# A three-stage transformer kernel on one core: second layer by block products, with its final sums folded into the last evictions, x differences kept in DRAM, w2's sums issued one per step, and weight conversion in order of use

## The chip, the cores and the metric

The kernel runs on one core of a Trainium2 chip. The metric is the device time of one execution in microseconds (us). Engines are named as in the profile: PE is TensorE (PEld its weight loads), DVE is VectorE, ACT is ScalarE, POOL is GpSimd, SP is SyncE, which here only issues DMAs; SPq is SP's queue of DMA issues.

## The reference, cut to what matters

Three parts follow each other; each one's output is the next one's input x.

```python
# 1 attention with random features, q k v of (4, 8, 576, 64)
x = num / den                                   # -> (2304, 512)
# 2 eight experts, dense, weighted by a balanced P (8 Sinkhorn turns on exp(x @ w_gate))
for e in range(8):
    h = np.maximum(x @ w1[e], 0.0)              # (2304, 512) @ (512, 1024)
    ye = h @ w2[e]                              # (2304, 1024) @ (1024, 512)
    out += P[:, e:e+1] * ye
# 3 one layer pair, weights given as float64
h = x @ w_in                                    # (2304, 512) @ (512, 2048)
out = (h - np.tanh(h)) @ w_out                  # (2304, 2048) @ (2048, 512)
```

## The kernel before

Every float32 operand is split into a high and a low part (`split`: ACT casts the high part, DVE or POOL subtracts it to get the low part), and a product is three matmuls of 128 rows by 384 or 512 columns. PE's program runs through the stages (0, 0), (0, 1), (0, 2) of part 2 and (1, 0), (1, 1), (1, 2) of part 3, each over 768 tokens. Stage (0, 0) loads w1 and w2, forms their sums and splits, and stores them in DRAM (`st1`, `st2`); later stages load them back.

**Stages (0, 1) and (0, 2)** take 32 steps Q each ("quads", numbered g = 0 to 63 over both). A quad multiplies 256 columns of one expert's w1 with x by seven block products (`product`, L1116: six matmuls each) and, between them, does the second layer of the quad before (`group`, L1281), also by seven block products: 42 matmuls on either side, 84 in a quad. `quad7` (L1186) calls `between(k)` after product k. That runs `slot(7 * g + k)`, in which the preloads of the next slot, the matmuls of this one, their evictions and the pieces `post(k)` are issued in this order; then it calls `tick` twice, which moves the background work on by a step: `weights` (loads, sums and splits of weights), `xops` (the next stage's x) and `convert`.

Each of the seven running sums `seven` (`xacc`) has two halves d. A group of matmuls adds to one half in one of two ways. With `act`, ACT preloads the half into a PSUM bank one slot ahead (L1286, named Y), the matmuls add to it, and ACT copies it back (L1304). Without, the matmuls start from zero (named X) and DVE adds the bank to the half (L1308). PSUM has four banks for groups (`lbank`) here. After the last quad of a stage `join` (L1316) adds the seven sums to the four blocks of the stage's output with DVE and POOL (L1321) and SP writes them to DRAM (`put`, L1325).

The second layer's left operand h is made on DVE (`gated`), cast by ACT (L1203) and its low part subtracted by POOL (L1206). In stage (0, 1) the first 32 quads also need fresh splits of w2's sums: `sums_of` (L208) issues four POOL operations in a row (L213 to L216).

**x** of the next stage is prepared by `xops` (L334): four blocks are loaded, differences formed by DVE (L361) and seven units split into a ring of eight tiles, most of them by DVE (L91), while the last quad of the stage frees them. At the end of stage (0, 0), `x2` (L1471) turns the output round in eight pieces: PE transposes, ACT copies to a tile of the ring `xo` (three buffers, also used by `keep`), and ACT issues the DMA.

**Conversion** of the float64 weights of part 3 (`convert`, L1058) takes jobs of 128 by 256 elements, the whole of w_in first, then w_out: a load by SP, six DVE operations, one of ACT and one of POOL, and a store. It runs in stage (0, 0), halts, and goes on in stage (0, 2). `fetch` (L189) loads converted weights only once all jobs are done (L192).

Of the kernel before, what the change touches and what calls it, by code (L numbers as in the profile page):

```python
# [20 lines left out]
def performer_moe_kernel(ctx, tc, q, k, v, omega, wg, w1, w2, win64, wout64, out):  # L21
# [6 lines left out]
    P = 128  # L28
# [38 lines left out]
    pd = dp.tile([NTT * E, P], F32, name="pd")  # L67

# [12 lines left out]


# [72 lines left out]
    def second_units(R):  # L155
# [6 lines left out]
        return units[:4] + [(0, R)] + units[4:] + [(6, R)] if r == NQ - 1 else units  # L162

    def weights():
# [3 lines left out]
        for Q in range(NQ):  # L168
            e, q = divmod(Q, NQE)
            jobs.append(("q", Q, lambda e=e, q=q: load_quad(e, q)))  # L170
            for f in (2 * q, 2 * q + 1):
                jobs.append(("s", 2 * Q + f % 2, lambda e=e, f=f: load_slab(w2[e][f * P : (f + 1) * P, :])))
        for g in range(NG + 1):
            jobs.append(("c", g, None))
        for s in range(NSB):
            for g in range(NGM):
                for f in range(g * GF, (g + 1) * GF, 2):
                    jobs.append(("i", 0, lambda f=f: load_win(f)))
                for f in range(g * GF, (g + 1) * GF):
                    jobs.append(("s", -1, lambda f=f: load_slab(wout32[f * P : (f + 1) * P, :])))  # L180
        ahead = []

        n_last = 3 * NGM * GF // 2 * NSB
# [5 lines left out]
        def fetch():  # L189
            while jobs and len(ahead) < 5:  # L190
                k = jobs[0][0]
                if len(jobs) <= n_last and not converted:  # L192
# [8 lines left out]
                k, a, f = jobs.pop(0)  # L201
# [6 lines left out]
        def sums_of(raws):  # L208
# [4 lines left out]
            G.tensor_tensor(s1, a21, a22, ALU.add)  # L213
            G.tensor_tensor(s2, s1, a11, ALU.subtract)
            G.tensor_tensor(s4, a12, s2, ALU.subtract)
            G.tensor_tensor(s3, a11, a21, ALU.subtract)  # L216
            return {1: s2, 2: s3, 3: s1, 5: s4}

        while ahead or jobs:
# [25 lines left out]
            elif k == "c":  # L245
                fresh = 0 < a <= NQ
                if a == 1:
                    send(9)
                    raws = slabs(0)
                    for _ in range(4):  # L250
                        yield 1
                    src = sums_of(raws)
                    yield None
                if fresh:
                    if a < NQ:
                        raws = slabs(a)
                    for _ in range(3):
                        yield 1
# [4 lines left out]
                for i in range(max(7, len(units))):  # L263
# [18 lines left out]
                    if fresh and (g < 0 or g == R and o in (1, 2, 3, 5)):  # L282
                        split(u, src[o], nc.vector if o == 2 else G)
                        store(st2[R][:, o], u)
# [5 lines left out]
                if fresh:  # L290
                    if a < NQ:
                        src = sums_of(raws)
# [36 lines left out]
    w2p, converted = [], []  # L329
# [4 lines left out]
    def xops():  # L334
        nx = 0
        order = []
        for k, (kind, s) in enumerate(stages):
# [18 lines left out]
            if kind == 0:  # L356
# [9 lines left out]
                subs = [do((0, 0), (0, 1), (0, 0)), do("t2", (1, 1), (0, 0)), do((0, 1), (1, 1), (0, 1))]  # L366
                last = [do("t2", (1, 0), "t2")]
                tiles = [(0, 0), "t2", (0, 1), (0, 0), (1, 0), (1, 1), "t2"]
                if opening:
                    load(0, 0)  # L370
                    load(1, 0)
                    yield None
                    plan = [0, 4, "rest", *subs[:2], 1, 3, subs[2], 2, 5, *last, 6]
# [18 lines left out]
                else:  # L392
                    for i, j in ((0, 0), (0, 1), (1, 1), (1, 0)):
                        load(i, j)
                    for _ in range(3):
                        yield None
                    seq = [(m, {0: subs, 1: last}.get(m)) for m in range(7)]
            else:
# [4 lines left out]
                seq = [(m, None) for m in range(4)]  # L403
            for m, then in seq:
                while not (len(order) < NX or order[len(order) - NX] in spentx):
                    yield 1
                unit(nx + m, b[tiles[m]], G if kind and m % 2 or not kind and m == 4 else V)
                yield None
                for f in then or ():
                    f()  # L410
                    yield None
            nx += len(seq)

    xdone = set()
# [6 lines left out]
    with ExitStack() as actx, tc.manual_schedule():  # L421
# [364 lines left out]
        for i in range(NUN):  # L786
            for r, items in enumerate(PLAN):
# [19 lines left out]
                if (i == 2 or i > 4) and r == SPL:  # L807
                    next(wprep, None)
# [900 lines left out]
```

## Time and profile before

| | us |
|---|---|
| median of 3 runs | 2172.45 (2170.06 to 2173.23) |
| profiled execution | 2173.33, of which the trace's span is 2171.5 |
| PE busy in the span | 2050.5 (94%) |
| PEld busy | 1908.8 (88%) |
| DVE busy | 1633.4 (75%) |
| POOL busy | 1498.8 (69%) |
| ACT busy | 1273.0 (59%) |

The stages follow each other in time: attention to about 190 us, stage (0, 0) to about 690, stage (0, 1) to about 1240, stage (0, 2) to about 1730, part 3 to the end. A busy share is a mean over all of them.

### The profile page before, as it was taken

The page shows a single profiled execution, that of the slowest core. Times are in us where ns is not written, and L with a number is a line of the kernel's source. Part 1 is how long each engine was busy: PE and PEld are TensorE (multiplying, and loading weights), DVE is VectorE, ACT ScalarE, POOL GpSimd, SP SyncE. Part 2 cuts the span into 40 slices and gives each one's busy share as a digit, 9 for nine tenths or more (in the row PEclk, how much of TensorE's full clock was granted, in tenths as well). Part 3 has the DMA queues.
Part 4 walks back from the last instruction along what each step waited for, and adds up shares of the span by engine and source line. Part 5 has one row for each costly group of instructions (what it writes and reads, how often), then busy time and mean ns, then how long its engine had stood idle before and what let it go on. Part 6 is the DMA issues. An engine that isn't in the chain of part 4 may idle for free.

```text
span 2171.5 us, 37317 instructions
## 1 busy us (share of the span) xinstructions
PE 2050.5 (94%) x11408; PEld 1908.8 (88%) x11408; DVE 1633.4 (75%) x3190; ACT 1273.0 (59%) x3110; POOL 1498.8 (69%) x1868
## 2 busy tenths in 40 slices
PE   9998999999999899999999869999999869999999
PEld 7776988899998799898998869899999869989998
DVE  8884868989876465666566657676777679999997
ACT  7883333344442355555555526666666668888885
POOL 7875877787873577777777657567676787666552
PEclk9999999999999899999999979999999989999999
DMA  6538778788865588787887578878888613222310
GB/s 171 132 101 291 270 258 288 256 285 278 281 244 192 181 289 284 254 295 264 259 296 263 197 239 277 308 265 285 304 290 301 238 70 106 80 96 78 106 41 34
DMA packets 343671, 475.03 MB, mean 219 GB/s; under 512 B 71200, under 2 KB 165040, under 8 KB 343472
## 3 DMA queue, kind: packets, MB, share of 16 engines
q1 hardware_dynamic: 337872, 466.04, 64.0%
q10 hardware_dynamic: 5600, 6.61, 0.9%
q8 instruction: 91, 1.49, 0.3%
q14 instruction: 108, 0.88, 0.1%
HBM read 332.48 MB, written 140.06 MB: 218 GB/s over the span
## 4 chain that ended last, share of the span: by engine, by line
PE 67%; DVE 9%; POOL 8%; DMA 8%; issue 4%; ACT 3%; SPq 1%; POOLq 0%; ACTq 0%; DVEq 0%
PE l L1429 18%; PE Y L1294 12%; PE b L1122 11%; PE e L1122 8%; PE a L1122 7%; PE p L1390 7%; PE X L1294 5%; DMA u<-st 2%; DMA st<-y 2%; POOL tmp L529 1%; POOL h L1206 1%; POOL eq L689 1%; DMA xd<-xo 1%; DVE seven L1308 1%; DVE t L1410 1%
## 5 line engine op out<-in xcount | busy, mean ns | idle before, releaser
L1429 PE MATMUL l<-v,h 128*128 128x512 f32 x2016 | 482.2, 392 | 2.0 <-ACT h L1133 0.8
L1429 PEld LDWEIGHTS l<-v,h 128*128 128x128 f32 x2016 | 376.4, 188 | 78.3 <-ACT h L1133 1.6
L1294 PE MATMUL Y<-h,y 128*128 128x384 f32 x1812 | 391.4, 344 | 47.8 <-POOL h L1206 32.2
L1294 PEld LDWEIGHTS Y<-h,y 128*128 128x128 f32 x1812 | 328.3, 194 | 58.4 <-POOL h L1206 39.0
L1122 PE MATMUL b<-x,u 128*128 128x384 f32 x1728 | 353.9, 340 | 17.1 <-DVE t L1216 16.3
L1304 ACT COPY seven<-Y 128x384 f32<-128x384 f32 x364 | 175.2, 481 | 311.0 <-PE Y L1294 309.5
L1206 POOL TENSOR_TENSOR h<-t,h 128x384 fp32r<-128x384 f32 x224 | 230.7, 1030 | 150.0 <-ACT h L1203 117.3
L1122 PEld LDWEIGHTS b<-x,u 128*128 128x128 f32 x1728 | 311.0, 191 | 22.9 <-DVE t L1216 16.6
L1206 POOL TENSOR_TENSOR h<-h,h 128x384 fp32r<-128x384 f32 x192 | 204.4, 1068 | 103.7 <-ACT h L1203 76.0
L1122 PE MATMUL a<-x,u 128*128 128x384 f32 x1152 | 234.6, 338 | 6.1 <-DVE h L1136 4.3
L1122 PE MATMUL e<-x,u 128*128 128x384 f32 x1152 | 238.3, 342 | 1.9 <-DVE t L1249 1.9
L1390 PE MATMUL p<-x,u 128*128 128x384 f32 x1152 | 212.6, 339 | 14.9 <-DVE seven L1308 8.9
L1390 PEld LDWEIGHTS p<-x,u 128*128 128x128 f32 x1152 | 205.0, 190 | 19.5 <-DVE seven L1308 9.2
L1122 PEld LDWEIGHTS a<-x,u 128*128 128x128 f32 x1152 | 205.0, 190 | 7.7 <-DVE h L1136 4.6
L1122 PEld LDWEIGHTS e<-x,u 128*128 128x128 f32 x1152 | 208.5, 193 | 2.4 <-DVE t L1249 2.4
L1294 PE MATMUL X<-h,y 128*128 128x384 f32 x876 | 191.1, 340 | 8.8 <-ACT h L1203 5.1
L91 POOL TENSOR_TENSOR v<-rs,v 128x256 fp32r<-128x256 f32 x176 | 143.9, 845 | 63.5 <-ACT v L88 53.5
L1418 POOL TENSOR_TENSOR h<-t,h 128x384 fp32r<-128x384 f32 x94 | 98.5, 1047 | 117.5 <-ACT h L1417 114.3
L1286 ACT COPY Y<-seven 128x384 f32<-128x384 f32 x364 | 176.3, 488 | 0.3
L1294 PEld LDWEIGHTS X<-h,y 128*128 128x128 f32 x876 | 157.1, 191 | 12.9 <-ACT h L1203 5.4
L1308 DVE TENSOR_TENSOR seven<-X,seven 128x384 f32<-128x384 f32 x256 | 135.7, 548 | 36.8 <-PE X L1294 36.7
L1203 ACT CAST h<-t 128x384 fp32r<-128x384 f32 x224 | 115.4, 515 | 62.8 <-POOL t L1259 30.0
(243 smaller groups left out, 3857.9 us busy)
## 6 DMA issues: line engine op xcount, KB each, us to landing
u<-st SPq DMA_DIRECT2D x448, 256.0 KB, 5.1
y<-st SPq DMA_DIRECT2D x336, 256.0 KB, 4.9
st<-u SPq DMA_DIRECT2D x224, 256.0 KB, 3.7
rs<-in_moe_w_dram SPq DMA_DIRECT2D x128, 256.0 KB, 4.3
st<-y SPq DMA_DIRECT2D x128, 256.0 KB, 5.6
st<-v SPq DMA_DIRECT2D x96, 256.0 KB, 5.0
rq<-in_moe_w_dram SPq DMA_DIRECT2D x32, 512.0 KB, 4.6
rqi<-win SPq DMA_DIRECT2D x24, 512.0 KB, 4.3
```

Source lines behind the costliest of these rows:

```text
L91: eng.tensor_tensor(dst[:, 1, i : i + w], src[:, i : i + w], dst[:, 0, i : i + w].bitcast(F32), ALU.subtract)
L529: nc.gpsimd.tensor_tensor(tmp[:, c], t[:, c], t[:, c], ALU.mult)
L1122: nc.tensor.matmul(ps[:, :TB], u[:, wi, c], x[:, xi, c], start=(start and m == 0), stop=(stop and m == 5), skip_group_check=True,)
L1203: nc.scalar.copy(H[k][:, 0], src)
L1206: eng.tensor_tensor(H[k][:, 1], src, H[k][:, 0].bitcast(F32), ALU.subtract)
L1286: nc.scalar.copy(cell[0], xacc[i][:, d])
L1294: nc.tensor.matmul(ps, uw[i, g][0][:, wi, d * P : (d + 1) * P], Hs[g][i][:, hi], start=(n == 0 and not cell), stop=(n == 3 * len(gs) - 1), ...
L1304: nc.scalar.copy(xacc[i][:, d], ps)
L1308: nc.vector.tensor_tensor(xacc[i][:, d], ps, xacc[i][:, d], ALU.add)
L1390: nc.tensor.matmul(ps, u1[f + i][:, wi, c], ux[state["x0"] + 2 * t + i][:, xi, c], start=(m == 0), stop=(m == 11))
L1418: nc.gpsimd.tensor_tensor(lo, s, hi.bitcast(F32), ALU.subtract)
L1429: nc.tensor.matmul(ps, hh[f][0][:, hi, t : t + P], u2[n + f][:, wi], start=(f == 0 and i == 0), stop=(f == len(hh) - 1 and i == 2),)
```

## The change

- **Second layer.** In `second_layer`, groups of half 0 and all first groups now go through ACT (`act` true): 194 groups that were X become Y, and rows of ACT go from 3137 to 3517, of DVE from 3192 to 3014. The last quad's groups get a list `outs`: their evictions are DVE additions of the PSUM bank and another running sum, so `join` only writes to DRAM. The 16 additions over 768 columns in the two joins (4 on DVE, 12 on POOL) go, and 40 over 384 columns on DVE come. The order of groups in the last quad changes.
- **Splits of h.** `hsplit(5)` and `hsplit(0)` are issued one product earlier.
- **w2's sums.** `sums_of` returns its four POOL operations, which are issued one per step. The low part of a split (`lower`) is issued one step after its cast.
- **x.** The four differences of stages (0, 1) and (0, 2) are formed early, stored in DRAM (`dd`), and the seven units are loaded one by one into the ring of five tiles; units 1, 3 and 5 are split by POOL. For each of these stages SP issues four more stores and seven more loads of 384 KB. `x2` uses this ring of five in place of `xo`.
- **Conversion.** Jobs come in the order in which part 3 uses them, and `fetch` waits only for the jobs that a load needs. In stage (0, 2) sixteen steps pass between the first load and its first use, and the pace is 26 steps in 32 ticks in place of 22.
- Two small matmuls of the gate use another ring of PSUM banks; attention sends stores at some of its steps.

```diff
-        if act and not first:
+        if (act or outs) and not first:
             at(t)[0].append(pre)
...
             def evict():
-                if act:
+                if outs:
+                    for x, y in outs:
+                        nc.vector.tensor_tensor(xacc[x][:, d], ps, xacc[y][:, d], ALU.add)
+                elif act:
                     nc.scalar.copy(xacc[i][:, d], ps)
...
-        def one(k, i):
+        def one(k, i, outs=()):
             first = r == 0
-            group(t + k, i, [R], 1, i in upper, first, False)
-            group(t + k, i, [R], 0, False, first, True)
+            group(t + k, i, [R], 1, first or i in upper, first, False, outs)
+            group(t + k, i, [R], 0, True, first, True, outs)
...
+        if r == NQ - 1:
+            one(1, 0)
+            two(2, 3, 5, [(5, 0)])
+            two(3, 6, 4, [(4, 0)])
+            one(4, 3, [(3, 0), (5, 5)])
+            one(5, 2, [(2, 0), (3, 3)])
+            one(7, 1, [(5, 5), (3, 3), (2, 2)])
+            one(8, 6, [(6, 2)])
+            join(s, t)
+            return
...
-        at(t + 4)[2].append(add(5, 3, G))
-        at(t + 5)[2].append(add(3, 2, G))
-        at(t + 6)[2].extend((add(4, 0, G), put(4, 0, 0)))
-        at(t + 7)[2].extend(
-            (add(1, 0, V), add(5, 1, V), put(5, 0, 1), add(3, 1, G), put(3, 1, 1), add(2, 1, G))
-        )
-        at(t + 8)[2].extend((add(6, 2, G), put(6, 1, 0), lambda: xdone.add((1, s))))
+        at(t + 6)[2].append(put(4, 0, 0))
+        at(t + 7)[2].extend((put(5, 0, 1), put(3, 1, 1)))
+        at(t + 8)[2].extend((put(6, 1, 0), lambda: xdone.add((1, s))))
...
         between(4)
+        hsplit(5, h22)
         product(b, 5, False, True, last)
...
         between(5)
-        hsplit(5, h22)
+        hsplit(0, h11)
         product(e, 6, False, True, last)
...
+                if a < NQ:
+                    src, todo = sums_of(raws)
+                    for f in todo:
+                        f()
                         yield None
...
+                for i, (dst, x, y) in enumerate(parts):
+                    minus(dst, x, y)
+                    yield None
+                    nc.sync.dma_start(dd[s - 1][i], b[dst])
...
+                    unit(nx + m, b[m], G if m % 2 else V)
+                    yield None
+                    if 0 < m < 3:
+                        fill(m + 4)
...
-                if len(jobs) <= n_last and not converted:
+                if jobs[0][3] > converted[0]:
                     break
...
         nx = ld()
-        yield
+        for _ in range(16 if fine else 1):
+            yield
...
-        x = xtp.tile([P, TB], F32, tag="xo", name="xo2", bufs=3)
+        while xbusy:
+            next(xprep)
+        x = xtp.tile([P, 2, TB], F32, tag="x", name="xo2")[:, 0]
```

**Place 1: POOL in quad 18 of stage (0, 1).** Rows h_18_5 and h_18_0 are low parts of h (the second number is its block), rows y are low parts of fresh w2 units, rows s are w2's sums. Before:

```order
L1206 TENSOR_TENSOR h_18_5_12923<-h_18_12867,h_18_5_12923 128x384
L91 TENSOR_TENSOR y_12941<-s,y_12941 128x256
L213 TENSOR_TENSOR s<-rs 128x256
L214 TENSOR_TENSOR s<-s,rs 128x256
L215 TENSOR_TENSOR s<-rs,s 128x256
L216 TENSOR_TENSOR s<-rs 128x256
L1206 TENSOR_TENSOR h_18_0_12949<-h_18_12887,h_18_0_12949 128x384
L1206 TENSOR_TENSOR h_18_3_13005<-t_18_12979,h_18_3_13005 128x384
```

and of the change:

```order
L1253 TENSOR_TENSOR h_18_5_12996<-h_18_12955,h_18_5_12996 128x384
L1253 TENSOR_TENSOR h_18_0_13017<-h_18_12978,h_18_0_13017 128x384
L241 TENSOR_TENSOR y_12913<-s,y_12913 128x256
L241 TENSOR_TENSOR y_13037<-s,y_13037 128x256
L238 TENSOR_TENSOR s<-rs 128x256
L238 TENSOR_TENSOR s<-s,rs 128x256
L238 TENSOR_TENSOR s<-rs,s 128x256
L1253 TENSOR_TENSOR h_18_3_13093<-t_18_13069,h_18_3_13093 128x384
```

The block h_18_0 has moved ahead of the sums; three sums and two low parts of y now stand ahead of h_18_3.

**Place 2: DVE at the start of stage (0, 2).** The names b, e, a with 32 to 34 are that quad's first-layer banks, t and h its temporaries, cw are the conversion's. Before, the conversion's first operation stands in the second quad of the stage:

```order
L1321 TENSOR_TENSOR seven_9437<-seven_9437,seven_9436 128x768
L1321 TENSOR_TENSOR seven_9441<-seven_9441,seven_9437 128x768
L1248 TENSOR_TENSOR t_32_15779<-b_32_15544,h_32_15660 128x384
L1249 TENSOR_TENSOR t_32_15780<-h_32_15630,b_32_15544 128x384
L1078 TENSOR_SCALAR cw_False<-r_36_15784 128x256
L1216 TENSOR_TENSOR t_7_33_15754<-b_33_15751,t_7_33_15753 128x384
```

and of the change, a quad later:

```order
L1263 TENSOR_TENSOR t_7_34_16089<-b_34_16086,t_7_34_16088 128x384
L1268 TENSOR_TENSOR t_7_34_16090<-b_34_16086,t_7_34_16088 128x384
L1269 TENSOR_TENSOR t_7_34_16090<-e_34_16087,t_7_34_16090 128x384
L1246 SCALAR_TENSOR_TENSOR h_34_16154<-t_7_34_16090,pb_0_15051 128x384
L1126 TENSOR_SCALAR cw_False<-r_36_15933 128x256
L1129 TENSOR_SCALAR cw_False<-cw_False 128x256
L1246 SCALAR_TENSOR_TENSOR h_34_16185<-a_34_16085,pb_0_15051 128x384
```

The first cw row, which waits for the load r, has moved from ahead of t_7_33 to behind three rows of quad 34.

**Place 3: ACT in the last quad of stage (0, 2).** Y and seven are the preloads and evictions named above (block, then half), h are casts. Before:

```order
L1286 COPY Y_2_1_21769<-seven_9438 128x384
L1304 COPY seven_9439<-Y_3_1_21738 128x384
L1203 CAST h_62_1_21780<-h_62_21574 128x384
L1286 COPY Y_1_1_21794<-seven_9437 128x384
L1304 COPY seven_9438<-Y_2_1_21769 128x384
L1203 CAST h_62_6_21805<-t_62_21783 128x384
```

and of the change:

```order
L1333 COPY Y_2_1_22011<-seven_9464 128x384
L1333 COPY Y_2_0_22013<-seven_9464 128x384
L1354 COPY seven_9465<-Y_3_1_21979 128x384
L1354 COPY seven_9465<-Y_3_0_21981 128x384
L1250 CAST h_62_1_22023<-h_62_21822 128x384
L1333 COPY Y_1_1_22036<-seven_9463 128x384
L1333 COPY Y_1_0_22038<-seven_9463 128x384
L1354 COPY seven_9464<-Y_2_1_22011 128x384
L1354 COPY seven_9464<-Y_2_0_22013 128x384
L1250 CAST h_62_6_22048<-t_62_22026 128x384
```

A slot with two groups now has two preloads and two evictions ahead of its cast, where it had one of each.

## Rows read from the trace of the kernel before

**Rows 1.** Chain of waits, PE: line, releaser: us in total, times, longest.

```profile
PE Y L1294 <- POOL h L1206: 32.2, 15, 3.4
PE b L1122 <- DVE t L1216: 16.3, 1, 16.3
PE Y L1294 <- ACT Y L1286: 14.9, 7, 5.0
PE p L1390 <- DVE seven L1308: 8.9, 1, 8.9
```

**Rows 2.** Windows: us, busy us (instructions) PE, PEld, DVE, ACT, POOL, PEclk, DMA, GB/s.

```profile
690.00:740.00 50.00, 42.12 (x212) 38.42 (x211) 23.67 (x45) 14.46 (x33) 18.20 (x21) 0.88 0.56 175
740.00:1205.00 465.00, 435.05 (x2397) 426.77 (x2396) 291.07 (x547) 255.67 (x626) 345.49 (x396) 0.97 0.82 274
1205.00:1280.00 75.00, 50.63 (x239) 48.36 (x238) 42.46 (x68) 25.40 (x56) 45.70 (x39) 0.77 0.60 203
1280.00:1450.00 170.00, 164.91 (x934) 163.81 (x933) 124.43 (x238) 106.73 (x252) 113.10 (x114) 0.98 0.80 274
1450.00:1700.00 250.00, 249.86 (x1441) 249.34 (x1440) 187.51 (x371) 166.99 (x399) 173.27 (x175) 1.00 0.84 296
1700.00:1785.00 85.00, 61.75 (x316) 58.50 (x315) 58.23 (x83) 53.53 (x127) 66.06 (x62) 0.90 0.38 129
```

**Rows 3.** Waits of PE from 740 to 1205 us.

```profile
PE Y L1294 <- POOL h L1206: 28.7, 14, 2.7
PE X L1294 <- DVE seven L1308: 0.4, 2, 0.2
```

**Rows 4.** Timeline of POOL: start, us, engine, line, operation [idle before, releaser].

```profile
879.64 0.74 POOL L213 TENSOR_TENSOR s<-rs 128x256 f32<-128x256 f32 x1
...
882.64 1.71 POOL L1206 TENSOR_TENSOR h<-h,h 128x384 fp32r<-128x384 f32 x1
```

**Rows 5.** Timeline of PE at the same place.

```profile
884.41 0.62 PE L1294 MATMUL Y<-h,y 128*128 128x384 f32 x2 [2.72 <-POOL h L1206]
...
885.92 2.12 PE L1294 MATMUL Y<-h,y 128*128 128x384 f32 x6
...
890.60 1.20 PE L1122 MATMUL a<-x,u 128*128 128x384 f32 x6
```

**Rows 6.** Timeline of ACT at the change to stage (0, 1).

```profile
707.77 0.48 ACT L1478 COPY xo<-x 128x384 f32<-128x384 f32 x1 [3.13 <-DMA xd<-xo]
...
717.87 0.48 ACT L1478 COPY xo<-x 128x384 f32<-128x384 f32 x1 [1.55 <-DMA xd<-xo]
```

**Rows 7.** Timeline of PE there.

```profile
716.00 0.69 PE L1294 MATMUL X<-h,y 128*128 128x384 f32 x1 [5.05 <-ACT h L1203]
...
720.93 2.29 PE L1122 MATMUL e<-x,u 128*128 128x384 f32 x6 [1.89 <-DVE t L1249]
```

**Rows 8.** Timeline of DVE at the change to stage (0, 2).

```profile
1267.94 0.29 DVE L1078 TENSOR_SCALAR cw_False<-r 128x256 f32<-128x256 f32 x1 [15.98 <-DMA r<-in_moe_w_in_dram]
```

**Rows 9.** Waits of SP's queue from 1200 to 1310 us.

```profile
SPq L1325 <- POOL seven L1321: 22.5, 2, 11.4
```

**Rows 10.** Timeline of PE at the change to part 3.

```profile
1734.90 4.58 PE L1390 MATMUL p<-x,u 128*128 128x384 f32 x12 [5.86 <-ACT u L88]
```

**Rows 11.** Timeline of DVE there.

```profile
1750.76 0.55 DVE L1410 SCALAR_TENSOR_TENSOR s<-t,s 128x384 f32<-128x384 f32 x1
...
1759.27 2.18 DVE L1410 SCALAR_TENSOR_TENSOR t<-t,t 128x384 f32<-128x384 f32 x1
...
1765.06 4.46 DVE L1321 TENSOR_TENSOR seven<-seven,seven 128x768 f32<-128x768 f32 x2
```

**Rows 12.** Groups of ACT and DVE, 1450 to 1700 us: busy us, mean ns, idle before.

```profile
L1286 ACT COPY Y<-seven 128x384 f32<-128x384 f32 x119 | 57.9, 487 | 0.0
L1304 ACT COPY seven<-Y 128x384 f32<-128x384 f32 x120 | 57.7, 481 | 65.8 <-PE Y L1294 65.8
...
L1308 DVE TENSOR_TENSOR seven<-X,seven 128x384 f32<-128x384 f32 x53 | 29.1, 549 | 8.5 <-PE X L1294 8.4
```

More of the change, by code (lines that the diff above doesn't have):

```diff
@@ L248, in weights @@
                     send(9)
[L249 to L253, printed above, removed]
+                if a < NQ:
+                    raws = slabs(a)
                 if fresh:
[L255 to L258, printed above, removed]
+                    yield 1
+                    yield 1
+                late = []
                 R = a - 1
@@ L282, in weights @@
                     if fresh and (g < 0 or g == R and o in (1, 2, 3, 5)):
-                        split(u, src[o], nc.vector if o == 2 else G)
-                        store(st2[R][:, o], u)
+                        nc.scalar.copy(u[:, 0], src[o])
+                        if late:
+                            late.pop()()
+                        late.append(lambda o=o, u=u: lower(R, o, u, src[o]))
                         yield None
@@ L327, in weights @@
             fetch()
-    w2p, converted = [], []
+    w2p = []
     ux = {}
@@ L372, in xops @@
                     yield None
+                    subs = [do((0, 0), (0, 1), (0, 0)), do("t2", (1, 1), (0, 0)), do((0, 1), (1, 1), (0, 1))]
+                    last = [do("t2", (1, 0), "t2")]
+                    tiles = [(0, 0), "t2", (0, 1), (0, 0), (1, 0), (1, 1), "t2"]
                     plan = [0, 4, "rest", *subs[:2], 1, 3, subs[2], 2, 5, *last, 6]
@@ L391, in xops, with fill @@
                     continue
[L392 to L397, printed above, removed]
+                for i, j in ((0, 0), (0, 1), (1, 1), (1, 0)):
+                    load(i, j)
+                for _ in range(3):
+                    yield None
+                parts = (
+                    ("t2", (0, 1), (0, 0)), ((0, 1), (1, 1), (0, 1)), ((1, 1), (1, 1), "t2"), ((1, 0), (1, 0), (1, 1))
+                )
+                for i, (dst, x, y) in enumerate(parts):
+                    minus(dst, x, y)
+                    yield None
+                    nc.sync.dma_start(dd[s - 1][i], b[dst])
+                yield None
+                yield None
+                side = lambda i, j: src[:, i, :, t0 + j * TB : t0 + (j + 1) * TB]
+                from_ = [side(0, 0), dd[s - 1][2], dd[s - 1][1], dd[s - 1][0], side(1, 0), side(1, 1), dd[s - 1][3]]
+                def fill(m):
+                    b[m] = xtp.tile([P, 2, TB], F32, tag="x", name=f"xm{m}")
+                    nc.sync.dma_start(b[m], from_[m])
+                xbusy.append(True)
+                for m in range(5):
+                    fill(m)
+                    yield None
+                for m in range(7):
+                    while not (len(order) < NX or order[len(order) - NX] in spentx):
+                        yield 1
+                    unit(nx + m, b[m], G if m % 2 else V)
+                    yield None
+                    if 0 < m < 3:
+                        fill(m + 4)
+                    yield None
+                xbusy.clear()
+                nx += 7
+                continue
             else:
@@ L402, in xops @@
                 tiles = [(0, 0), (1, 0), (0, 1), (1, 1)]
-                seq = [(m, None) for m in range(4)]
-            for m, then in seq:
+            for m in range(4):
                 while not (len(order) < NX or order[len(order) - NX] in spentx):
                     yield 1
-                unit(nx + m, b[tiles[m]], G if kind and m % 2 or not kind and m == 4 else V)
+                unit(nx + m, b[tiles[m]], G if m % 2 else V)
                 yield None
[L409 to L412, printed above, removed]
+            nx += 4
+    xbusy = []
     xdone = set()
@@ L1279, in slot, with group @@
         plan.pop(t)
-    def group(t, i, gs, d, act, first, last):
+    def group(t, i, gs, d, act, first, last, outs=()):
         cell = []
@@ L1367, in second_layer @@
             one(6, 6)
-        elif r == NQ - 1:
-            one(3, 0)
-            one(8, 6)
-            join(s, t)
     pbs = []
```

83 lines of the change are left out of this document (46 added, 37 removed).

## The prediction

> **What bounds the kernel now.** I read the waits of PE first. PE is busy for most of the span, so what can be won is its idle time and the time in which it ran slowly. Four lines lead [rows 1]: groups of the second layer wait 32.2 us in 15 places for POOL's low parts, one product waits 16.3 us for DVE, groups wait 14.9 us for ACT's preloads, and the first products of part 3 wait 8.9 us for DVE's last evictions.
>
> Then the windows, to see where these lie [rows 2]. From 1450 to 1700 us, inside stage (0, 2), PE is busy 249.86 of 250 us and 1441 matmuls are recorded: 0.1735 us each. That is what PE does when nothing is late, and 84 of them make a quad of 14.6 us. From 740 to 1205, inside stage (0, 1), 2397 matmuls of the same kind take 465 us, 0.1940 each: 2397 x 0.0205 = 49 us are lost. The changes of stage lose more per us: 239 matmuls in 1205 to 1280 are worth 41.5 of 75 us (33 lost), and PE idles 7.9 us in 690 to 740 and 23.3 us in 1700 to 1785. The part from 1280 to 1450 loses 8.
>
> A stall costs more than itself. After the 2.72 us wait at 884.41 a group's six matmuls take 2.12 us, where 1.20 is usual [rows 5], and the granted clock of that stretch's window is 0.97, at the change to stage (0, 2) 0.77 [rows 2]: PE works at the lower of its two levels for some us after each. In 740 to 1205 the waits sum to 29.1 us [rows 3], so of the 49 some 20 are the clock's.
>
> **w2's sums and the earlier splits of h (term D).** Ahead of the stall at 884.41 POOL works through the four sums, from 879.64 on, and starts the late h only at 882.64 [rows 4]; PE's group starts when that h is done [rows 5]. This repeats in every second quad, 14 times in the window [rows 3]: the block of h that two quads share (h_0) stands behind the sums. The order shows it moved ahead of them, and cast a product earlier. The sums are now ahead of h_3, whose consumer comes some slots later: two low parts and three sums at 0.74 us [rows 4] are 3.7 us, nearly two slots of 2.08 us (14.6 / 7), and each h takes POOL about 1 us more. I see room, but little: POOL is busy 345.5 of the 465 us, so over 28.5 quads 12.1 us each, 83% of 14.6. Bounds: 49 us if the stage runs as (0, 2) does, 10 us if h_3 and its followers are late instead. I take 39, four fifths, nearer to the upper end because the moved row is the one that PE waited for.
>
> **DMA.** A faster stage must move its bytes faster. 465 us at 274 GB/s are 127.4 MB [rows 2]; the stage's eleven new x transfers of 384 KB add 4.3 MB. In 426 us that is 309 GB/s; the highest mean that a full-speed window shows is 296. If 296 were the ceiling, the window could not be shorter than 131.7 MB / 0.296 = 445 us, and D would be 20. The Trainium skill, "DMA: Bandwidth & Descriptors", section "Where 436 GB/s comes from", sets the limit of HBM at about 358 GB/s for a core; by that page the same bytes need 368 us and D is not touched by DMA. No row here shows where the ceiling is, so the 20 stays as a rival.
>
> **More groups through ACT.** Each quad has three groups more that cost ACT a preload and an eviction, 0.487 + 0.481 us, and DVE 0.549 us less [rows 12]. ACT's busy time per quad rises by 2.9 us: in 1450 to 1700 from 167 us by 17.2 quads x 2.9 = 50 to 217 of 250; in 740 to 1205 from 9.0 to 11.9 of 14.6 a quad. It stays under PE's time, and the preload of the next slot is issued ahead of this slot's matmuls, so PE's product and groups (2.08 us a slot) cover it. I take nothing for it either way. What it does without that cover: two preloads late by 0.487 each put 0.97 us on a slot with two groups, three such slots a quad. The Trainium skill, "Perfetto Trace Analysis", section "Optimizing Scalar/DVE Operations", advises moving work to ScalarE when VectorE is saturated. DVE is busy 187.5 of 250 here, so by that page the move has no reason; by these rows its price is nothing as well, and the sum is the same unless ACT comes late, which is the slow rival below. DVE's 1.6 us less in a quad is worth nothing by itself, since nothing from 740 to 1205 waited for DVE.
>
> **Change to stage (0, 1), term A.** ACT's copies of x2 wait for the DMA of three copies before, from 707.77 to 717.87 [rows 6], and the casts behind them come so late that PE idles 5.05 and 1.89 us and restarts at the lower clock, six matmuls in 2.29 us [rows 7]. DVE's `keep` tiles of the same ring wait too. With five buffers the fourth and fifth copy wait for nothing, `keep` has its own ring, and three copies still wait. Bounds 4 (the waits of the last three stay) and 13.9 (7.9 idle plus 0.12 x 50 us of clock, [rows 2]); I take 8. The forced steps of x ahead of x2 are units that PE needs some slots later anyway; they cost nothing while their ACT casts fit there.
>
> **Change to stage (0, 2), term B.** DVE's first conversion operation waits 15.98 us for its load [rows 8], and PE's next product waits 16.3 us for the DVE row behind it [rows 1]. The load was late because SP's queue had stood before `put`, which waited for POOL's additions, 22.5 us in two waits [rows 9]. The change takes away both: sixteen steps, about a quad, lie between load and first use, and `put` waits only for DVE's evictions. The 33 us lost from 1205 to 1280 also hold one stall of D's kind and a DVE backlog from x units. New there: twenty additions of 0.549 us on DVE in one quad, 11 us beside its usual 10.2 a quad (291 / 28.5), above 14.6. So DVE runs late for a few us and some waits stay. Bounds 11 and 33, I take 20: the 16.3 and most of the clock it cost.
>
> **Change to part 3, term C.** PE waits 5.86 us for the first part 3 weights and then works twelve matmuls in 4.58 us [rows 10], where 2.1 is full speed: 8 us. Their load was issued only after the last conversion; now it needs four early jobs, and conversion itself runs 26 / 22 as fast, so it ends before the last quads. After that PE idles behind DVE: its chain takes 2.18 us for an operation that takes 0.55 alone, and two additions of the join take 4.46 us, with POOL's additions beside them [rows 11]. Those four or more go, but DVE gets its twenty. Bounds 5 and 23, I take 12.
>
> **The rest** is put at nothing. The 8 us from 1280 to 1450 hold a 5.0 us wait for a preload [rows 1], behind an x cast of part 3, which the change leaves. Units of x on POOL (three in place of one) are covered by the join's six additions of POOL that go in the same quads. Differences formed early take DVE the same time in the middle of a stage. Stores in attention only leave earlier.
>
> **Sum.** D 39 + A 8 + B 20 + C 12 = 79 us. The profiled execution took 2173.3 us, 1.8 more than its span and 0.9 above the median of the runs; less 79 that is 2094.3, and against the median 2093.4. I predict **2093 us**.
>
> **The rivals.**
> - *POOL or DMA keeps stage (0, 1) slow* (chance 0.17). For it: 83% and in-order waits, and 309 against 296 GB/s. Against: h_0 alone was waited for. D is 10 to 20: 2114 to 2123 us.
> - *The changes of stage stay stalled* (0.12): DVE's twenty additions, or SP's queue, take the place of the wait removed. For it DVE's 21 us of work in a quad of 14.6; against it, PE's banks can lag a slot or two. B 8, C 2: 2116.
> - *All of it is won* (0.10): D 49, A 13, B 33, C 20 make 115: 2058.
> - *Slower* (0.06): ACT's preloads become what PE waits for, in the three slots a quad with two groups, 186 of them in 62 quads. From 79 / 186 = 0.42 us a slot, less than one preload, the gain is gone; at 0.97 us, two preloads, 180 us are added: 2274. Against it: none of the 14.9 us of such waits lies in 740 to 1205 [rows 3], and none can be in 1450 to 1700, where PE is idle for 0.14 us.
> - *The change does not do what it says* (0.04): stalls only move by a slot and the time stays at 2173; ends 3 in 100 within the bound, 1 slower.
>
> The forecast itself, 2080 to 2108, has 0.51. **Range** 2058 to 2130: it takes in the first three rivals to their ends, and leaves about 0.15 outside. A measurement of this kernel can tell about 0.2% (4.3 us) from no change. Faster 0.51 + 0.17 + 0.12 + 0.10 = 0.90, same 0.03, slower 0.07.
>
> **What the changed profile would show.** D: waits of groups for POOL's h from 32 us to under 10, and 280 or more matmuls per 50 us in stage (0, 1) (258 now, 50 / 0.1940). A: no ACT wait for a DMA of xo above 2 us. B: no wait of DVE for r, and the 16.3 us gone. C: no wait of PE for the first u of part 3. ACT: 217 of 250 us in stage (0, 2), with PE still busy throughout. Wrong would be: waits of Y groups for ACT's preloads inside the stages, h_3 in place of h_0 behind POOL, a DMA releaser inside stage (0, 1), or PE waiting at the changes for DVE's `outs` additions.

## The result and the profile after

The changed kernel takes 2084.84 us (median of 4 runs, 2081.79 to 2085.71), the kernel before 2172.84 in the runs beside it: a ratio of 0.9591, 95% interval 0.9572 to 0.9610, or 88 us less, where 79 were forecast. The profiled execution took 2085.71 us, its span is 2083.6.

**Where PE waits now.** The waits of PE in the kernel after, in the columns of [rows 1]:

```profile
PE Y L1341 <- ACT Y L1333: 18.3, 10, 4.6
...
PE X L1341 <- ACT h L1250: 7.0, 1, 7.0
PE X L1341 <- POOL h L1253: 3.5, 5, 1.3
...
PE Y L1341 <- POOL h L1253: 1.4, 2, 0.8
```

Of the four lines of [rows 1] three are gone or nearly: 32.2 us behind POOL are 1.4 (with 3.5 more in X groups), and the 16.3 behind DVE's `t` and the 8.9 behind its last evictions no longer appear. What is left of the waits for POOL's h lies at the changes of stage: between 722 and 1133 us, inside stage (0, 1), there is none. The preloads of ACT are a longer wait than before, 18.3 for 14.9, and at the change to stage (0, 2) a wait of 7.0 us for ACT's cast of h is new.

**Windows** of the kernel after, in the columns of [rows 2]: two long stretches of stages (0, 1) and (0, 2), and the three places that still lose.

```profile
745.00:1145.00 400.00, 399.66 (x2306) 399.37 (x2306) 252.25 (x445) 311.07 (x770) 334.30 (x385) 1.00 0.91 317
1150.00:1210.00 60.00, 48.93 (x257) 46.56 (x256) 34.77 (x63) 30.06 (x69) 33.63 (x34) 0.91 0.80 265
1210.00:1400.00 190.00, 182.51 (x1031) 181.29 (x1030) 131.65 (x243) 148.59 (x360) 126.51 (x127) 0.98 0.83 287
1400.00:1650.00 250.00, 248.29 (x1426) 246.68 (x1425) 166.30 (x304) 206.05 (x501) 174.68 (x176) 1.00 0.80 281
1650.00:1700.00 50.00, 39.98 (x202) 37.47 (x202) 37.00 (x62) 38.75 (x92) 36.87 (x40) 0.93 0.33 111
```

Stage (0, 1) runs at 400 / 2306 = 0.1735 us a matmul, the figure that stage (0, 2) showed before [rows 2]. At that rate nothing is left to win there. Stage (0, 2) is no longer without waits: 1426 matmuls in 250 us, 1441 before.

**Gain by stretch.** PE's program of products is the same in both kernels, so the start of one and the same product or group can be read in the two timelines of PE. What lies between two such marks is a stretch.

| mark in PE's program | before | after | gain of the stretch ahead of it | forecast |
|---|---|---|---|---|
| first transpose of x2 | 697.29 | 694.76 | 2.5 | none |
| first group in the third quad of stage (0, 1) | 734.91 | 721.77 | 10.6 | A 8 (4 to 13.9) |
| fourth product of the second last quad of stage (0, 1) | 1195.61 | 1133.15 | 49.3 | D 39 (10 to 49) |
| first group in the third quad of stage (0, 2) | 1284.60 | 1204.69 | 17.5 | B 20 (11 to 33) |
| fourth product of the last quad of stage (0, 2) | 1718.95 | 1644.61 | -5.6 | 0 |
| first group l of part 3 | 1784.86 | 1694.27 | 16.3 | C 12 (5 to 23) |
| end of the span | 2171.5 | 2083.6 | -2.7 | none |

The marks between the first and the end, as PE's timeline of the kernel before has them, and below as that of the kernel after has them:

```profile
734.91 1.20 PE L1294 MATMUL X<-h,y 128*128 128x384 f32 x6
...
1195.61 1.20 PE L1122 MATMUL b<-x,u 128*128 128x384 f32 x6
...
1284.60 1.20 PE L1294 MATMUL X<-h,y 128*128 128x384 f32 x6
...
1718.95 1.20 PE L1122 MATMUL b<-x,u 128*128 128x384 f32 x6
...
1784.86 2.92 PE L1429 MATMUL l<-v,h 128*128 128x512 f32 x12
```

```profile
721.77 1.20 PE L1341 MATMUL X<-h,y 128*128 128x384 f32 x6
...
1133.15 1.20 PE L1169 MATMUL b<-x,u 128*128 128x384 f32 x6
...
1204.69 1.20 PE L1341 MATMUL X<-h,y 128*128 128x384 f32 x6
...
1644.61 1.20 PE L1169 MATMUL b<-x,u 128*128 128x384 f32 x6
...
1694.27 2.92 PE L1477 MATMUL l<-v,h 128*128 128x512 f32 x12
```

The stretches sum to 87.9 us, the difference of the spans. A, B and C lie inside their bounds and D just above its upper one. What was put at nothing lost 5.6 us.

**The new wait at the change to stage (0, 2).** Timeline of ACT, then of PE, at that place:

```profile
1194.77 0.86 ACT L1354 COPY seven<-X 128x384 f32<-128x384 f32 x2 [10.65 <-DMA xd<-seven]
1195.51 0.52 ACT L1250 CAST h<-h 128x384 fp32r<-128x384 f32 x1
```

```profile
1187.92 1.21 PE L1169 MATMUL b<-x,u 128*128 128x384 f32 x6
1196.09 0.69 PE L1341 MATMUL X<-h,y 128*128 128x384 f32 x1 [6.97 <-ACT h L1250]
```

ACT's copy writes the first group of the new stage into running sum 3, which `put` is still storing; it waits 10.65 us for that DMA. The cast of h stands behind it in ACT's queue, and PE's group needs that h.

**The wait in stage (0, 2).** The same two timelines at 1320 us:

```profile
1320.48 0.83 ACT L106 CAST x<-xt 128x768 fp32r<-128x768 f32 x1 [4.19 <-DMA xt<-xd]
```

```profile
1322.16 2.29 PE L1341 MATMUL Y<-h,y 128*128 128x384 f32 x6 [4.62 <-ACT Y L1333]
```

The first x cast of part 3 is issued before its load has landed, and a preload stands behind it. It is the wait of 5.0 us of the kernel before.

PE's waits for preloads in stage (0, 2) come to 9.1 us. The other 9.2 of the 18.3 us lie in its last quad, where ACT already has operations of part 3 in its queue ahead of the preloads. The longest of these:

```profile
1678.09 4.21 PE L1341 MATMUL Y<-h,y 128*128 128x384 f32 x12 [4.47 <-ACT Y L1333]
```

### The profile page after: what moved, and what is told of

The parts are those of the page before. It is cut to its first block, busy times and chain, and to the rows that moved or that the text cites. A ratio compares the mean times of both kernels' runs of the same rounds, so it can differ in the third digit from the quotient of the medians.

```text
span 2083.6 us, 37583 instructions
## 1 busy us (share of the span) xinstructions
PE 2021.4 (97%) x11408; PEld 1888.0 (91%) x11408; DVE 1560.0 (75%) x3012; ACT 1418.5 (68%) x3490; POOL 1475.6 (71%) x1864
## 4 chain that ended last, share of the span: by engine, by line
PE 78%; DVE 5%; POOL 5%; DMA 4%; ACT 3%; issue 3%; SPq 1%; ACTq 0%; POOLq 0%; DVEq 0%
PE l L1477 20%; PE Y L1341 18%; PE b L1169 13%; PE e L1169 9%; PE a L1169 9%; PE p L1438 7%; PE X L1341 2%; POOL tmp L581 1%; DMA xt<-xd 1%; POOL h L1253 1%; POOL eq L741 1%; DMA u<-st 1%; DMA y<-st 1%; DMA st<-y 1%; DVE jk L728 0%
## 5 line engine op out<-in xcount | busy, mean ns | idle before, releaser
L1341 PE MATMUL Y<-h,y 128*128 128x384 f32 x2394 | 489.8, 337 | 19.8 <-ACT Y L1333 18.3
L1341 PEld LDWEIGHTS Y<-h,y 128*128 128x128 f32 x2394 | 423.2, 189 | 25.0 <-ACT Y L1333 22.7
L1169 PE MATMUL b<-x,u 128*128 128x384 f32 x1728 | 348.2, 336 | 1.3 <-DVE t L1263 1.0
L1354 ACT COPY seven<-Y 128x384 f32<-128x384 f32 x534 | 247.0, 481 | 139.8 <-PE Y L1341 136.3
L1169 PEld LDWEIGHTS b<-x,u 128*128 128x128 f32 x1728 | 305.0, 188 | 6.8 <-DVE t L1263 1.3
L1333 ACT COPY Y<-seven 128x384 f32<-128x384 f32 x558 | 262.9, 488 | 6.2 <-DVE seven L1352 6.2
L1169 PE MATMUL e<-x,u 128*128 128x384 f32 x1152 | 234.0, 338 | 0.0
L1268 DVE TENSOR_TENSOR t<-b,t 128x384 f32<-128x384 f32 x64 | 35.6, 557 | 123.2 <-PE b L1169 123.1
L1512 DVE SCALAR_TENSOR_TENSOR acc<-l,pt,acc 128x512 f32<-128x512 f32 x144 | 104.8, 744 | 30.3 <-PE l L1477 28.6
L106 ACT CAST u<-s 128x256 fp32r<-128x256 f32 x128 | 49.3, 409 | 98.7 <-POOL u L109 33.4
```

The lines of the kernel that those rows point to most:

```text
L106: nc.scalar.copy(dst[:, 0], src)
L1169: nc.tensor.matmul(ps[:, :TB], u[:, wi, c], x[:, xi, c], start=(start and m == 0), stop=(stop and m == 5), skip_group_check=True,)
L1333: nc.scalar.copy(cell[0], xacc[i][:, d])
L1341: nc.tensor.matmul(ps, uw[i, g][0][:, wi, d * P : (d + 1) * P], Hs[g][i][:, hi], start=(n == 0 and not cell), stop=(n == 3 * len(gs) - 1), ...
L1354: nc.scalar.copy(xacc[i][:, d], ps)
L1512: V.scalar_tensor_tensor(a, ps, p[:, e : e + 1], a, ALU.mult, ALU.add)
```

## The experiments

All are made from the changed kernel, by undoing one part or, in the last set, by removing one wait. "Differs by" is the difference of the ratios to the kernel before (0.9591 for the changed kernel) times 2172.8 us. Each ratio's interval is about 0.0015 to either side, so a difference of less than about 5 us is not resolved: by their times alone e1, e2 and i5 cannot be told from the changed kernel.

| run | median us | ratio (95%) | differs by |
|---|---|---|---|
| e1 sums in a row | 2086.36 | 0.9603 (0.9588 to 0.9617) | +2.6 |
| e2 h split late | 2083.67 | 0.9592 (0.9578 to 0.9606) | +0.2 |
| e3 both | 2127.40 | 0.9792 (0.9776 to 0.9808) | +43.7 |
| e4 groups on DVE | 2091.34 | 0.9628 (0.9614 to 0.9643) | +8.0 |
| e5 join by additions | 2096.24 | 0.9648 (0.9632 to 0.9663) | +12.4 |
| e6 conversion after one step | 2095.69 | 0.9649 (0.9631 to 0.9668) | +12.6 |
| e7 loads wait for all jobs | 2092.52 | 0.9633 (0.9618 to 0.9648) | +9.1 |
| e8 x2 in three tiles | 2093.89 | 0.9640 (0.9625 to 0.9654) | +10.6 |
| i1 x cast later | 2079.34 | 0.9565 (0.9552 to 0.9578) | -5.6 |
| i2 block in sum 1 | 2075.60 | 0.9554 (0.9535 to 0.9572) | -8.0 |
| i5 two jobs ahead | 2081.66 | 0.9573 (0.9560 to 0.9586) | -3.9 |
| i4 all three | 2064.93 | 0.9496 (0.9483 to 0.9509) | -20.6 |

"By the marks" means that the stretches of the table above were read in the run's own timeline of PE. This is how much longer each stretch is than in the changed kernel, in us. Runs that leave a stretch alone differ in it by up to 2.7. i2 is left out, for the reason given with it.

| run | x2 to the third quad of (0, 1) | stage (0, 1) | change to (0, 2) | stage (0, 2) | change to part 3 | part 3 |
|---|---|---|---|---|---|---|
| e3 both | +2.2 | +43.3 | -0.7 | -0.9 | -0.3 | +0.5 |
| e4 groups on DVE | -0.5 | +1.1 | -1.2 | +7.7 | +0.1 | +0.5 |
| e5 join by additions | +0.3 | +0.1 | +5.7 | -0.4 | +7.2 | -0.8 |
| e6 conversion after one step | +1.1 | +1.3 | +3.9 | +6.5 | -1.3 | +0.1 |
| e7 loads wait for all jobs | -0.2 | +1.3 | +0.5 | -8.0 | +16.0 | +1.0 |
| e8 x2 in three tiles | +10.1 | +0.1 | -0.6 | +0.9 | -0.7 | +0.6 |
| i1 x cast later | +0.5 | -0.1 | -0.7 | -3.1 | -0.1 | -2.8 |
| i5 two jobs ahead | +2.4 | +0.3 | -0.2 | -2.6 | -0.5 | +0.1 |
| i4 all three | +2.4 | +0.1 | -8.8 | -6.6 | -0.8 | -2.6 |

**Term D: e1, e2 and e3.** My theory was that h_0 behind POOL's sums cost the 49 us; the rival that the spreading of the sums did, or DVE's and ACT's relief.

```diff
 # e1; e3 has it too
-                    for f in todo:
-                        f()
-                        yield None
+                    for f in todo:
+                        f()
+                    for f in todo:
+                        yield None
 # e2; e3 has it too
         between(4)
-        hsplit(5, h22)
         product(b, 5, False, True, last)
...
-        hsplit(0, h11)
+        hsplit(5, h22)
         product(e, 6, False, True, last)
...
         between(6)
+        hsplit(0, h11)
         high(4, h21)
```

> The changed kernel, with w2's four sums issued in a row again, in the same four steps; h_0 stays ahead of them. Theory (what cost 49 us in stage (0, 1) was that h_0 stood behind POOL's sums): nothing comes back, 2080 to 2092 us, and PE waits for POOL's h under 10 us in all. Rival (the spreading made the gain: four sums in a row are 3.0 us of POOL in front of h_3): 15 such quads stall by 1 to 2 us with as much lost to the clock, 2110 to 2135 us.

> The changed kernel, with hsplit(5) and hsplit(0) issued where they were before; the sums stay one per step. In POOL's order one sum stands between the low parts of y and h_0 where four stood, so h_0 comes 0.74 x 3 = 2.2 us earlier than in the kernel before, whose stalls were 2.0 us on average. Theory (place of h_0 alone): the stalls shrink to 0 to 1 us, 2090 to 2110 us, with waits for POOL's h of 5 to 15 us. Rival (spreading the sums is all that mattered): no stall, 2080 to 2090 us.

> The changed kernel with both undone: sums in a row and h_5 and h_0 split at their old places; the groups through ACT, conversion, x and joins stay. Theory (POOL's order was the whole of the gain in stage (0, 1)): 49 to 55 us come back, 2134 to 2140 us, and waits of groups for POOL's h of 25 to 32 us. Rival (part of the gain came from DVE's or ACT's relief or the transfers): 2095 to 2125 us.

e1 is where the theory put it; e2 is where the rival put it, and e1 rules that rival out. Either half of the edit is enough alone, and only both undone bring the stalls back. PE's waits of e3 from 725 to 1180 us:

```profile
PE Y L1342 <- POOL h L1254: 30.1, 15, 2.7
```

They are those of [rows 3] (28.7 us, 14 times), and the time returns by 43.7, so h_0's place behind all four sums is shown as the cause of most of D. It falls short of the 49 to 55 expected: between the second and third mark e3 takes 454.7 us (721.66 to 1176.35), the kernel before 460.7, the changed one 411.4. The other 6.0 us are not waits (30.1 us in e3, 29.1 in the kernel before) but PE's own time: for the same work of this stretch it is busy 424.6 us in e3 and 430.8 in the kernel before, at granted clocks of 0.98 and 0.97. Which other part of the change makes PE run less of it slowly was not tried.

**Groups through ACT: e4.**

```diff
-            group(t + k, i, [R], 1, first or i in upper, first, False, outs)
-            group(t + k, i, [R], 0, True, first, True, outs)
+            group(t + k, i, [R], 1, i in upper, first, False, outs)
+            group(t + k, i, [R], 0, False, first, True, outs)
```

> The changed kernel with the 194 groups of half 0, and the first groups, taken back from ACT to DVE (the last quads' folded additions stay). Theory (a move between two engines that nobody waits for is worth nothing): 2081 to 2089 us, matmuls in stage (0, 1) at 286 or more in 50 us. Rival 1 (DVE's relief was needed): 1.6 us a quad more on DVE make PE wait, 2095 to 2130. Rival 2 (the ACT evictions at the start of stage (0, 2), which stood 10.7 us behind the stores of the sums, cost PE its 7.0 us and the clock): 2072 to 2079.

The time lies between theory and rival 1. Stage (0, 1) stays at full speed (290 or 291 matmuls in most windows of 50 us). What is lost lies in stage (0, 2). PE's waits there, 1300 to 1640 us, and ACT's:

```profile
PE Y L1341 <- ACT Y L1333: 12.8, 8, 4.6
```

```profile
ACT h L1250 <- DVE t L1246: 25.1, 16, 5.9
```

In the changed kernel ACT waits 15.7 us for this `t` in the same stretch, and PE 9.1 for the preloads. So DVE's relief is worth something where the conversion runs: DVE is late with t, ACT's cast of h stands waiting, and the preload behind it is late for PE. That chain is read from these waits and was not tried by itself. Rival 2 is not tried by this run either: half 1 of sum 3 stays with ACT in stage (0, 2), as it was in the kernel before, and ACT's first copy there still waits for the store, with PE 6.5 us behind it:

```profile
1193.36 0.48 ACT L1354 COPY seven<-X 128x384 f32<-128x384 f32 x1 [11.18 <-DMA xd<-seven]
```

i2 below tries it.

**Folding the join: e5.**

```diff
-        if r == NQ - 1:
-            one(1, 0)
-            two(2, 3, 5, [(5, 0)])
...
-            join(s, t)
-            return
...
+        at(t + 4)[2].append(add(5, 3, G))
+        at(t + 5)[2].append(add(3, 2, G))
+        at(t + 6)[2].extend((add(4, 0, G), put(4, 0, 0)))
...
```

> The changed kernel with the join done by separate additions again (4 on DVE, 12 on POOL over 768 columns), the last quad's groups in the old order. Theory (the folding is what cleared SP's queue and DVE and POOL at both changes): the stores wait for POOL some 20 us again, and PE waits for DVE's last evictions at the change to part 3; 4 to 8 us come back at the change to stage (0, 2), 6 to 12 at the change to part 3, 2095 to 2104 us. Rival (40 additions more on DVE, and ACT's evictions behind the stores, cost what the folding saves): 2079 to 2089.

The theory's time. By the marks 5.7 us come back at the change to stage (0, 2) and 7.2 at the change to part 3. SP's queue there, 1150 to 1225 us, and PE at the change to part 3:

```profile
SPq L1375 <- POOL seven L1371: 13.7, 1, 13.7
```

```profile
1694.78 5.42 PE L1440 MATMUL p<-x,u 128*128 128x384 f32 x22 [5.47 <-ACT seven L1354]
```

The store stands behind POOL again, as in [rows 9], and PE behind the last evictions.

**The sixteen steps: e6.**

```diff
-        for _ in range(16 if fine else 1):
-            yield
+        yield
```

> The changed kernel with one step between the conversion's first load and its first use in stage (0, 2), where sixteen pass. Theory (the load was late because SP stood before the stores, which now leave at 1178 to 1186 us): DVE waits 5 to 10 us for the load, but in the same stretch in which PE waits 7.0 us for ACT, so only 0 to 5 us are added, 2083 to 2090 us. Rival (the sixteen steps made term B): DVE waits 12 us or more and PE for DVE behind it, 2096 to 2105.

Here my theory fails and the rival's time is met but for 0.3 us. SP's queue and DVE at the change to stage (0, 2):

```profile
1186.05 1.46 SPq L1115 DMA_DIRECT2D r<-in_moe_w_out_dram  x2
1198.92 0.38 SPq L1370 DMA_DIRECT2D xd<-seven  x1
```

```profile
1197.21 0.29 DVE L1125 TENSOR_SCALAR cw_False<-r 128x256 f32<-128x256 f32 x1 [13.38 <-DMA r<-in_moe_w_out_dram]
1197.42 0.55 DVE L1262 TENSOR_TENSOR t<-b,t 128x384 f32<-128x384 f32 x1
```

Though SP issues the load with no wait before it, it takes some 11 us to land beside the stores of 384 KB, and DVE stands for it. Behind it stand `t`, for which PE waits 12.7 us, and the last additions of the join, for which SP's last store waits (1198.92). The wait does not hide in PE's 7.0 us, it takes their place and is longer.

This change of stage is only 3.9 us longer by the marks. Another 6.5 us are lost in stage (0, 2), where PE's wait behind the first x cast of part 3 grows from 4.62 to 7.91 us, because ACT waits longer for that load:

```profile
1331.94 0.83 ACT L106 CAST x<-xt 128x768 fp32r<-128x768 f32 x1 [7.60 <-DMA xt<-xd]
```

Why that load is later there was not tried.

**Loads of part 3: e7.**

```diff
-                    jobs.append(("i", 0, lambda f=f: load_win(f), NCV if s else made["i", f]))
+                    jobs.append(("i", 0, lambda f=f: load_win(f), NCV))
...
-                            NCV if s else made["o", f],
+                            NCV,
...
-                    pace[4] = 26
+                    pace[4] = 22
```

> The changed kernel, but converted weights are loaded only when all jobs are done, and conversion goes 22 steps in 32 ticks in place of 26; the jobs stay in the new order. Theory (term C, the late first load of part 3's weights): PE waits 4 to 7 us for the first u of part 3 and loses 2 to 4 to the clock, 2090 to 2096 us. Rival (the loads were never what held the change to part 3, DVE's chain was): 2082 to 2088.

The theory's time, but as the rest of two larger things. The wait is twice what I expected:

```profile
PE p L1438 <- ACT u L106: 13.1, 1, 13.1
```

It also takes away part of what the kernel after waits for a few us later (Y for ACT's preloads, 9.2 us in 1640 to 1760, here 5.6). By the marks the change to part 3 is 16.0 us longer, and stage (0, 2) is 8.0 us shorter. There, from 1210 to 1635 us, PE waits once:

```profile
PE Y L1341 <- ACT Y L1333: 3.7, 1, 3.7
```

The first load of part 3's weights is issued at 1638.40 us in the changed kernel and at 1655.10 in e7, when the stage is all but over or over. So the 8.0 us are the price of the faster pace, 26 steps in 32 ticks, and not of the loads. How the 16.0 us divide between pace and loads was not tried, since e7 undoes both.

**x2: e8.**

```diff
-        while xbusy:
-            next(xprep)
-        x = xtp.tile([P, 2, TB], F32, tag="x", name="xo2")[:, 0]
+        x = xtp.tile([P, TB], F32, tag="xo", name="xo2", bufs=3)
```

> The changed kernel with the copies of x2 in the ring of three tiles again, shared with keep, and no steps of x forced ahead of them. Theory (term A): ACT's copies wait for the DMA of three copies before, PE idles 5 to 7 us and restarts slowly, 2092 to 2097 us. Rival (the earlier casts of h and first evictions by ACT already took the wait away): 2083 to 2088.

As the theory said, for the ring and the forced steps together. DVE's `keep` tile waits for the copies' DMA, and PE for DVE (2.48 us) and for ACT's copies (3.63):

```profile
714.23 0.56 DVE L1296 TENSOR_TENSOR t<-h,b 128x384 f32<-128x384 f32 x1 [11.01 <-DMA xd<-xo]
```

**Three waits removed: i1, i2, i5, i4.** These go on from the waits that the profile after shows.

```diff
 # i1, in xops, part 3
                     load(i, j)
-                yield None
+                for _ in range(3):
+                    yield None
 # i2
-        at(t + 7)[2].extend((put(5, 0, 1), put(3, 1, 1)))
+        at(t + 7)[2].extend((put(5, 0, 1), put(1, 1, 1)))
...
-            one(7, 1, [(5, 5), (3, 3), (2, 2)])
+            one(7, 1, [(5, 5), (1, 3), (2, 2)])
 # i5, in convert
-        nx = ld()
+        nx = [ld() for _ in range(2 if fine else 1)]
...
-        while nx:
-            (r, dst), nx = nx, ld()
+        while nx[0]:
+            r, dst = nx.pop(0)
+            nx.append(ld())
```

> The changed kernel, with the first x cast of part 3 issued two background steps (some 16 us) later after its load. Theory (what stage (0, 2) lost at 1322 us is ACT standing 4.2 us for that load, with the preloads behind it): the 4.6 us wait of PE goes, with its clock, 5 to 7 us in all, 2077 to 2081 us. Rival (ACT's in-order casts wait for DVE there anyway): 2083 to 2087.

> The changed kernel, with the fourth output block summed up in running sum 1 in place of 3, so that the next stage's first group, which writes sum 3, no longer overwrites a tile that a store still reads; sum 1 is written two slots (4.2 us) later. Theory (PE's 7.0 us at the change to stage (0, 2) come from ACT's evictions behind the stores): ACT's wait of 10.7 us falls to 5 to 7, PE's to 2 to 4, and 4 to 6 us are won, 2078 to 2082 us. Rival (DVE or POOL are as late there, ACT's wait only covers theirs): 2083 to 2087.

> The changed kernel, with the conversion of stage (0, 2) loading two jobs ahead in place of one. Theory (DVE's 8.2 us of waits for loads of the conversion stand in front of h, and ACT's preloads behind h, as at 1389 us): PE's waits in stage (0, 2) fall from 9.1 us by 3 to 4, and 3 to 5 us are won, 2079 to 2083 us. Rival (a longer line of loads only delays others in SP's queue): 2084 to 2090.

> The changed kernel with the three edits of this set together: x cast later, fourth block in sum 1, conversion two jobs ahead. If the three waits are separate, the gains add up to 12 to 18 us: 2067 to 2073 us. If they share a cause (ACT's queue is late for whatever reason), the sum falls short: 2074 to 2080.

The times of i1 and i5 lie where their theories put them. i1's does so in part for another reason: by the marks stage (0, 2) is 3.1 us shorter, since the wait of 4.62 us goes and one of 1.79 for DVE's `t` comes, and part 3 is 2.8 us shorter. The edit also moves the x casts of part 3's later stages, and there a wait of PE for ACT's h falls from 2.01 to 0.24 us. In i5 the wait of 2.80 us at 1389 us falls to 0.31. i2 wins more than expected. Its profiled execution was the longest of its four runs (2084.09), so only its waits are used. ACT's at the change, 1140 to 1225 us:

```profile
ACT seven L1354 <- DMA xd<-seven: 5.9, 2, 4.0
```

10.65 us in one piece have become 5.9 in two, and PE's wait for that h is gone. In i4, with the three edits together, PE's waits from 1216 to 1630 us are

```profile
PE Y L1343 <- ACT Y L1335: 3.4, 5, 1.3
```

and the gain is not below the sum of the three (5.6 + 8.0 + 3.9 = 17.5, measured 20.6, 2 us beyond the expected range). As far as these times can tell, the three waits are separate. i4 beats both kernels, 2064.93 us.

## Why the prediction was right

- **D** (forecast 39, measured 49.3 by the marks) was right in mechanism and too small. I kept ten us back for h_3 behind three sums. Inside the stretch PE no longer waits for POOL's h at all, and it does not in e1 either, which puts a fourth sum ahead of h_3: the room of "nearly two slots" was enough. Of the 49.3 us, 29.1 were waits. PE's busy time for the same work fell from 430.8 to 411.0 us, so the "some 20" that I laid to the clock were right too. The DMA rival falls: stage (0, 1) moved 317 GB/s over 400 us, so 296 was only what had been asked for. The page of the Trainium skill that the prediction named, "DMA: Bandwidth & Descriptors", section "Where 436 GB/s comes from", sets the limit at about 358 for a core; the trace passes it over 25 us, and the measurement decides. In the columns of [rows 2]:

```profile
850.00:875.00 25.00, 25.00 (x146) 25.00 (x145) 18.69 (x32) 19.20 (x48) 22.56 (x26) 1.00 1.00 364
```

  PE loses nothing in this window, but the DMA engines are busy throughout it, and one wait of PE in the stage, of 0.34 us at 835 us, is for a DMA, which I had named as a sign against me. Little room is left there.
- **A** (8, measured 10.6; e8 gives 10.6 back, 10.1 by the marks) held as worked out. One ACT wait for the copies' DMA is left, 1.8 us, under the 2 that I named.
- **B** (20, measured 17.5) came out near, with a step in it wrong. I laid the late load to SP's queue alone. In the kernel before, the load is issued here:

```profile
1259.21 0.93 SPq L1068 DMA_DIRECT2D r<-in_moe_w_in_dram  x2
```

  It takes 8.7 us to land, more than half of DVE's 15.98 us [rows 8]. e6 shows the same: the load is slow by itself beside the stores, and the sixteen steps had to cover it. The stall that remains is not DVE's twenty additions, as I expected, but ACT's first eviction into sum 3 behind the store that still reads that sum (i2). The move of groups to ACT did not make it: ACT had half of this eviction before, and the stall stays in e4. The prediction does not ask which sum the next stage writes first. By the marks e5 and e6 give back 5.7 and 3.9 us at this change; the other 8 of B are not traced to one part.
- **C** (12, measured 16.3): both halves are there. By the marks e7 gives back 16.0 us at this change (loads and pace) and e5 7.2 (join), together more than C, so they overlap. Of the bounds I took a value too near the middle.
- **ACT's groups "nothing either way"** failed in two ways. e4 shows them worth some 8 us in stage (0, 2), against the sentence that DVE's 1.6 us a quad are worth nothing by itself; that sentence was read from stage (0, 1), where it holds. And PE did wait for preloads inside stage (0, 2), which I had named as a sign against me. ACT's busy time, 206 of 250 us, is under the 217 forecast, and in e7 ACT is as busy in that stage (189 of 230 us for 188) with one such wait left, so it was order, not load. The page of the Trainium skill, "Perfetto Trace Analysis", section "Optimizing Scalar/DVE Operations", names a saturated VectorE as the case for such a move. DVE was not saturated (187.5 of 250 us [rows 2]), and e4 shows the move paid all the same. The slow rival did not come: no such wait lies in stage (0, 1).
- **The rest "at nothing"** was -5.6 in stage (0, 2), and this is the term that was wrong. The wait for the x cast stayed, as said (4.6 us for 5.0), and four smaller ones came, 4.5 us together, one of 2.8 behind a conversion load for which DVE stood 3.2 us, where I had said that DVE would wait for none. I had counted on the faster conversion in C and given it no price; e7, which takes the pace back, has none of the four and wins 8.0 us in this stage. i1 and i5 remove the two longest waits; 3.4 us of small ones are left in i4. The 2.7 us that part 3 lost are a wait of the same kind, for x casts issued ahead of their loads: i1 and i4, which issue them later, win 2.8 and 2.6 back.

That the sum came within 9 us is in part luck: D and C were too low by 10 and 4 us, and stage (0, 2) lost 6 that I had not counted. The parts undone one by one give back 96 us, more than the 89 of the whole. They overlap, e5 and e7 above all, at the change to part 3 (23.2 us for 16.3), and e4 and e6 lose 14 us in stage (0, 2), where the change as a whole won nothing. Open are the 6 us of D that e3 does not return and about 8 of B.

## What to carry to other kernels

Where an in-order engine holds up another, look for the one instruction that is waited for and what stands ahead of it: moving it, or thinning what is ahead, did the same work, and either would have done. Price an instruction by what its output tile waits for, and by who is queued behind it, as well as by its own time: a sum that a store still reads held ACT for 10.65 us, and writing another sum first won some 8 us (i2). Background work that is made faster to be ready in time takes its time from the stage that it runs in: the pace that goes with the win at the change to part 3 cost 8.0 us ahead of it (e7). Give a load that is issued beside large stores its own slack in steps, since a free queue does not make it land soon.

## What the runs showed that was not expected

A conversion load's median time from issue to landing in the changed kernel is 4.6 us for w_out and 4.7 for w_in; the first one of stage (0, 2), of w_out and issued between the join's stores, took 10.1, and in the kernel before the first one took 8.7. With DVE waiting, in e6, it made a stall of 12.7 us out of a queue that was free.
